# Attention with 32 memory slots and capacity routing on one Trainium2 core: scores and gate products by 64x32 tiles, softmax by groups of up to two units, a written-out order of the front part, and the routing's branch turned round

## The chip, the cores and the metric

The kernel runs on one core of one Trainium2 chip. Its time is the device time of one execution in microseconds. Before the change the median of three runs is 603.41 us (602.47 to 606.62).

## The reference

Eight batches, eight heads, 576 positions, 64 channels, 32 memory slots. First the attention with memory slots, then a mixture of eight experts on its result (4608 rows of 512):

```python
a = exp(phi - max(phi, axis=2)); a = a / sum(a, axis=2)     # over the 576 positions
k_m = einsum('bhsm,bhsd->bhmd', a, k)                       # 32 slots per head
v_m = einsum('bhsm,bhsd->bhmd', a, v)
attn = softmax(q @ k_m.T / 8)                               # over the 32 slots
x = (attn @ v_m) -> rows (b, s) of 8*64 channels
logits = x @ w_gate                                         # 4608 x 8
for (row, expert) in descending order of logit:             # greedy, 576 rows per expert
    if the row is free and the expert has room: assign
out[rows of e] = relu(x[rows of e] @ w1[e]) @ w2[e]
```

## The kernel before

The program has a **front** (attention and routing) and an **expert part**. The front works in eight batches and 18 units. A batch loads phi and the keys and values, takes the exponentials of phi (`ex`), multiplies them with keys and values into 32 slots per head (`kv_`), normalises (`zn`, `zs`), transposes the slots (`kt`), copies them to SBUF (`kb`, `vd`) and multiplies the value slots with the gate weights (`vg`, `vl`), so that logits come with the attention's product. A unit is 256 positions of one batch, or (units 8 and 17) the last 64 positions of four batches. Its steps are: load of the queries (`load_q`), scores on TensorE (`SC`, PE L982), transpose (`T1`, DVE L987), maximum (`MX`, L990), subtraction (`SB`, POOL L993), exponential (`SE`, ACT L996), sums and reciprocal (`SU`, L1000 and L1001), multiplication (`NM`, POOL L1004), transpose (`T2`, DVE L1009), product with the value slots (`AV`, PE L1017), a separate product for the logits of units 13 to 17 (`LG`, `LC`), copies from PSUM (`XC`, ACT L1035), and the write of x to DRAM (`ST`, SP L1044 and L1048).

The scores contract 64 channels. Before, the slots lie in zero-padded tiles of 128 rows (`kbd`), so that both halves of the positions use all 128 rows of the array in 128x32 tiles.

The routing finds thresholds from the logits (L107 to L157), a mask and an assignment (L171 to L178, one-hot `oh`), positions by a scan (L187), and 36 blocks of comparisons `L` (LP on POOL L210, LV on DVE L212, LS on ACT L214), whose product (`ll`, L228) gives row numbers; `ix` (L231, L232) writes them to `idx`. A flag tells whether a slower routing (`rest`) is needed; all engines read it and branch (L292, L293). Then POOL gathers the first expert's 640 rows (L412), five at 128 rows each, and TensorE transposes them (L447) and begins the first expert (L470).

The first expert's weights are loaded in the front as eight tiles of 512 KB: four of w1 (`w1a`, SP L371) and four of w2 (`w2a`, L404). Each is split into two fp32r parts: the high one by a cast on ACT (L374, L405), the low one by a subtraction on POOL (L377, L406). The tiles have four buffers (`st`), and the gathered rows use these too.

What order each engine runs the front in is set by a planner (`build` and `Sched.order`): each step has an engine, a duration, a key and the steps that it needs; a simulated run picks steps by key, and the kernel issues them in the order of the simulated starts. Every engine runs its own queue strictly in order. The expert part has a planner of its own, which the change leaves alone.

Of the kernel before, what the change touches and what calls it, by code (L numbers as in the profile page):

```python
# [66 lines left out]
class Router:  # L67
# [106 lines left out]
    def assign(s):  # L174
# [3 lines left out]
        nc.vector.tensor_tensor(s.oh.rearrange("p e t -> p t e"),m,v[:,:,None].to_broadcast([128,NT,E]),op=ALU.is_ge)  # L178
# [111 lines left out]
    def finish(s):  # L290
        nc=s.nc; tc=s.tc
        rv=nc.values_load(s.flag[0:1,0:1],min_val=0,max_val=E)  # L292
        with tc.If(rv>0):  # L293
# [42 lines left out]
class FFN:  # L336
# [70 lines left out]

    def gather(s,xd,idx,i):
        c=s.cols(0)[i]
        if i%2==0: s.g0=s.sp.tile([128,1024],F32,name="st")  # L410
# [1 line left out]
        s.nc.gpsimd.indirect_dma_start(out=g,out_offset=None,in_=xd,in_offset=bass.IndirectOffsetOnAxis(ap=idx[:,c:c+1],axis=0))  # L412
# [310 lines left out]
def build(X,f,B=8):  # L723
# [9 lines left out]
    for n in range(N):
        T=anch[n]+X['UB'][n]; b,bb,_=units[n]; rem=len(bb)>1
        op('SP',(1.32,3.4),T+X['SC']+X['lq'],lambda n=n:f.load_q(n),[],[('lq',n)],[('Q',X['NQ'],('Q',n))])
        for h in range(2):
# [4 lines left out]
        op('ACT',.68,T+X['SE'],lambda n=n:f.SE(n),[('sb',n)],[('se',n)],[],[('p',n)])
        op('DVE',1.05,T+X['SU'],lambda n=n:f.SU(n),[('se',n)],[('su',n)],[],[('p',n)])
        pool=X['NP']>>(n%2)&1
        op('Pool' if pool else 'DVE',1.13 if pool else .97,T+X['NM'],lambda n=n,e=pool:f.NM(n,e),[('su',n)],[('nm',n)],[],[('p',n)])
        op('DVE',.74,T+X['T2'],lambda n=n:f.T2(n),[('nm',n)],[('t2',n)],[('pTd',len(X['DF']),('pT',n)) if n in X['DF'] else ('pT',2,('pT',n))],[('p',n)])
# [403 lines left out]
```

## Time and profile before

| what | value |
|---|---|
| profiled execution, whole | 603.53 us |
| its span, first to last instruction | 601.8 us |
| mean granted TensorE clock | 0.971 |
| TensorE busy | 546.1 us (91%) |
| VectorE, ScalarE, GpSimd busy | 394.5, 286.9, 257.9 us |
| bytes moved by DMA | 116.58 MB |
| first gather for the first expert | at 172.13 us |
| first product of the first expert | at 181.25 us |

The 1.7 us between span and whole execution lie around the program. Times in the views are microseconds from the first instruction. In a timeline row come the start, the length, the engine, the line, the operation, output and inputs, and in brackets the idle time before it with what ended it. PE is TensorE, DVE VectorE, ACT ScalarE, POOL GpSimd, SP the queue that issues DMAs.

### The profile page before, as it was taken

To read this page: it belongs to the slowest core of one execution; us is meant where nothing else is said; L and a number is where in the kernel's file an instruction comes from. 1 tells how busy PE (TensorE), PEld (TensorE's weight loads), DVE (VectorE), ACT (ScalarE), POOL (GpSimd) and SP (SyncE) were. 2 spreads that over 40 slices of the span, in tenths; PEclk is the share of its full clock that TensorE was granted. 3 is DMA by queue.
4 is the path that set the end of the run, shared out by engine and by line. 5 is a ranking of instruction groups with operands and counts; after the bars stand their busy time and mean duration, and the time that the engine had idled before them with its cause. 6 is when DMAs were issued, how large, how long until landed. Compare 5 with 4: busy or idle time off the path is not lost.

```text
span 601.8 us, 11305 instructions
## 1 busy us (share of the span) xinstructions
PE 546.1 (91%) x4344; PEld 453.7 (75%) x4344; DVE 394.5 (66%) x738; ACT 286.9 (48%) x577; POOL 257.9 (43%) x244
## 2 busy tenths in 40 slices
PE   8988889665867999999899989999999999999996
PEld 3666666463236988998688879889889889989984
DVE  3486866561722251536888958988897898898800
ACT  2375654614302342443557445646646656754511
POOL 6164544863347325559233431542362182282003
PEclk9999999957989799999999989999999999999999
DMA  8999999842129967895861264152346327315002
GB/s 315 421 414 359 409 355 382 301 139 106 36 81 325 316 218 251 295 287 209 245 188 38 69 210 142 53 204 86 114 129 212 97 70 254 96 35 203 1 0 80
DMA packets 48269, 116.58 MB, mean 194 GB/s; under 512 B 6352, under 2 KB 20304, under 8 KB 46160
## 3 DMA queue, kind: packets, MB, share of 16 engines
q1 hardware_dynamic: 41584, 94.29, 45.5%
q0 software_dynamic: 6624, 21.50, 9.8%
q8 instruction: 36, 0.59, 0.4%
q14 instruction: 25, 0.20, 0.1%
HBM read 87.45 MB, written 28.31 MB: 192 GB/s over the span
## 4 chain that ended last, share of the span: by engine, by line
PE 42%; issue 13%; DMA 8%; POOL 4%; ACT 2%; DVE 2%; SPq 1%; POOLq 0%; DVEq 0%; ACTq 0%
PE ph L482 18%; PE ph L501 16%; PE ph L470 5%; DMA xsort<-xu,pi 3%; POOL out L506 2%; PE ph L490 2%; DMA xu<-xd 2%; DMA out<-y,idx 1%; DMA st<-in_moe_w 1%; POOL xsort L431 1%; PE ph L447 1%; SPq L439 1%; DVE w1l L391 1%; DMA g<-xsort 1%; DMA st<-xd,idx 1%
## 5 line engine op out<-in xcount | busy, mean ns | idle before, releaser
L501 PE MATMUL ph<-w2h,hh 128*128 128x512 f32 x256 | 101.5, 397 | 0.0
L501 PE MATMUL ph<-w2h,hl 128*128 128x512 f32 x256 | 101.4, 396 | 0.0
L501 PE MATMUL ph<-w2l,hh 128*128 128x512 f32 x256 | 101.1, 395 | 0.0
L506 POOL DMA_INDIRECT out<-y,idx x32 | 41.0, 1280 | 92.4 <-ACT y L503 86.4
L501 PEld LDWEIGHTS ph<-w2l,hh 128*128 128x128 f32 x256 | 48.1, 188 | 11.7
L501 PEld LDWEIGHTS ph<-w2h,hh 128*128 128x128 f32 x256 | 48.1, 188 | 11.3
L501 PEld LDWEIGHTS ph<-w2h,hl 128*128 128x128 f32 x256 | 48.1, 188 | 11.1
L503 ACT COPY y<-ph 128x512 f32<-128x512 f32 x32 | 18.8, 587 | 64.6 <-PE ph L501 48.4
L431 POOL DMA_INDIRECT xsort<-xu,pi x36 | 35.7, 992 | 27.3 <-DMA xu<-xd 16.8
L482 PE MATMUL ph<-xh,w1h 128*128 128x288 f32 x192 | 41.9, 299 | 3.2 <-ACT p L562 3.1
L383 POOL TENSOR_TENSOR st<-st 128x512 f32<-128x512 f32 x24 | 41.5, 1735 | 7.2 <-ACT s1h L390 2.5
L473 DVE SCALAR_TENSOR_TENSOR hl<-ph,hh 128x288 fp32r<-128x288 f32 x56 | 24.1, 450 | 30.9 <-ACT hh L472 17.2
L383 POOL TENSOR_TENSOR st<-s,st 128x512 f32<-128x512 f32 x12 | 18.7, 1562 | 58.7 <-DVE w1l L391 32.8
L473 DVE SCALAR_TENSOR_TENSOR hl<-cc,hh 128x288 fp32r<-128x288 f32 x72 | 39.8, 573 | 6.1 <-ACT hh L472 5.7
L482 PE MATMUL ph<-xh,w1l 128*128 128x288 f32 x192 | 41.6, 298 | 0.0
L482 PE MATMUL ph<-xl,w1h 128*128 128x288 f32 x192 | 41.2, 296 | 0.0
L472 ACT ACTIVATE hh<-ph 128x288 fp32r<-128x288 f32 x56 | 21.6, 410 | 38.4 <-PE ph L470 15.4
L391 DVE TENSOR_TENSOR w1l<-st,w1h 128x512 fp32r<-128x512 f32 (+1 forms) x24 | 34.5, 1444 | 4.8 <-issue 4.8
L405 ACT CAST w2h<-st 128x1024 fp32r<-128x1024 f32 x32 | 33.4, 1046 | 7.4 <-DMA st<-in_moe_w 6.2
L406 DVE TENSOR_TENSOR w2l<-st,w2h 128x1024 fp32r<-128x1024 f32 x28 | 34.0, 1217 | 4.2 <-ACT w2h L405 3.3
L383 POOL TENSOR_TENSOR s<-st 128x512 f32<-128x512 f32 x12 | 17.2, 1438 | 43.7 <-DMA st<-in_moe_w 39.6
L472 ACT ACTIVATE hh<-cc 128x288 fp32r<-128x288 f32 x72 | 30.3, 443 | 10.1 <-DVE cc L484 10.1
(194 smaller groups left out, 1326.5 us busy)
## 6 DMA issues: line engine op xcount, KB each, us to landing
st<-in_moe_w SPq DMA_DIRECT2D x64, 512.0 KB
kv<-in_kv SPq DMA_DIRECT2D x16, 1161.0 KB
qm<-in_q SPq DMA_DIRECT2D x18, 512.0 KB
xd<-xs SPq DMA_DIRECT2D x16, 512.0 KB
xu<-xd SPq DMA_DIRECT2D x16, 512.0 KB
g<-xsort SPq DMA_DIRECT2D x96, 64.0 KB
pt<-in_phi SPq DMA_DIRECT2D x8, 576.0 KB
xd<-xs SPq DMA_DIRECT2D x8, 128.0 KB
```

The lines of the kernel that those rows point to most:

```text
L383: s.nc.gpsimd.tensor_tensor(o,x,y,op=ALU.subtract if i else ALU.add)
L391: def wlo(s,e,c,i): h,l,x=s.wop(e,c,i); s.nc.vector.tensor_tensor(l,x,h,op=ALU.subtract)
L405: def l2b(s,j): s.nc.scalar.copy(s.w2h[j],s.R2[j])
L406: def l2c(s,j,pool=False): (s.nc.gpsimd if pool or j in WP else s.nc.vector).tensor_tensor(s.w2l[j],s.R2[j],s.w2h[j],op=ALU.subtract)
L431: i=s.nc.gpsimd.indirect_dma_start(out=xs,out_offset=bass.IndirectOffsetOnAxis(ap=pi[:,t:t+1],axis=0),in_=s.X[n][:,a],in_offset=None)
L470: for j in js: nc.tensor.matmul(ph[j][:,:288],w,x[:,2*j+k//2,k%2],start=(i==0),stop=(i==11))
L472: def rh(s,f,j,c): s.nc.scalar.activation(s.hh[:,f,j],c[:,:288],AF.Relu)
L473: def rl(s,f,j,c): s.nc.vector.scalar_tensor_tensor(s.hl[:,f,j],c[:,:288],0.0,s.hh[:,f,j],op0=ALU.max,op1=ALU.subtract)
L482: s.nc.tensor.matmul(c[:,:288],s.W(w,a)[:,k,m],x[:,b,k],start=start and n==0,stop=n==5,skip_group_check=not start); n+=1
L501: nc.tensor.matmul(py,a[:,f,j,o],b,start=(f==0 and q==0),stop=(f==7 and q==2))
L503: def full_y(s,c,py): s.Y[c]=y=s.yp.tile([128,D],F32,name="y"); s.nc.scalar.copy(y,py)
L506: i=s.nc.gpsimd.indirect_dma_start(out=out,out_offset=bass.IndirectOffsetOnAxis(ap=ix,axis=0),in_=s.Y.pop(c)[:n],in_offset=None)
```

## The change

The slots are copied once, unpadded (`kvt`), and scores, gate products and the last 64 rows of phi's product use tiles of 64 rows and 32 columns. `vd` and the padded buffers go. The softmax steps MX, SB, SE, SU, NM and T2 work on groups of one or two units (`GRP`). Some copies and splits move to DVE (`ALT`), the POOL blocks of `L` go (`RV=[27,0,9]`: DVE, POOL, ACT). The loads of w2 now need the last group's NM, and their casts the last group's SE. The planner's order is replaced by a table of 514 numbers. The gathers move into the branch that is taken when the flag is zero, ahead of the large `RV`; twelve warm-up products before the gathered rows go. The core of the diff:

```diff
 class Sched:
+ORDER=(285,286,288,264,289,290,306,291,292,287,293,294,309,73,310,267,
...
+504,510,)
-    AVS=194.9, SU=21.38, NM=60.47, XC=86.9, LO=-19.41, ST=-61.43, EV=11, NP=3, NB=7, NQ=9, NK=2,
+    AVS=194.9, SU=21.38, NM=60.47, XC=86.9, LO=-19.41, ST=-61.43, EV=11, NP=3, NB=6, NQ=8, NK=2,
-    CF=323.04, CB=630.67, NA=2, BD=[1, 2, 3, 5, 7], DF=[13, 14, 15, 16, 17], LG=272.42, LC=-601.61, DA=519.47,
-    DX=160.21, DS=404.52, R0=251.98, RK=-1728.94, W1=-59.3, WH=341.28, WS=227.46, WE=0, W2=-50, WB=100, RV=[22, 6, 8], la=-57.61,
+    CF=323.04, CB=630.67, NA=2, BD=[0, 1], DF=[13, 14, 15, 16, 17], LG=272.42, LC=-601.61, DA=519.47,
+    DX=160.21, DS=404.52, R0=251.98, RK=-1728.94, W1=-59.3, WH=341.28, WS=227.46, NX=3, NU=3, GRP=[[2],[3],[1,0],[5,10],[8,6],[4,12],[11,7],[9],[14,16],[13,15],[17]], ALT=(('xc',2,0),('xc',2,1),('nm',1),('xc',15,1),('xc',17,1),('w1c',1),), W2=-50, WB=100, RV=[27, 0, 9], la=-57.61,
-        op('SP',(1.32,3.4),X['W2']+i,lambda j=j:f.w2a(j),[('w1a',3)],[('w2a',j)],[('st',4,('s2',j))])
-        op('ACT',1.1,X['W2']+X['WB']+i,lambda j=j:f.w2b(j),[('w2a',j)],[('w2b',j)],[],[('s2',j)])
+        op('SP',(1.32,3.4),X['W2']+i,lambda j=j:f.w2a(j),[('w1a',3),('nm',len(X['GRP'])-1)],[('w2a',j)],[('st',4,('s2',j))])
+        op('ACT',1.1,X['W2']+X['WB']+i,lambda j=j:f.w2b(j),[('w2a',j),('se',len(X['GRP'])-1)],[('w2b',j)],[],[('s2',j)])
-        seq=S_.order(X['slack'])
+        seq=S_.fixed(ORDER) if ORDER else S_.order(X['slack'])
...
         def SC(n,hh):
-            for u in range(2):
-                for m,bb in enumerate(bs):
-                    for i in range(4):
-                        nc.tensor.matmul(sc[32*i:32*i+32,u,hh,w*m:w*m+w],KBD[ks[bb]][:,4*hh+i,u,:],qT[:,4*hh+i,w*m:w*m+w],start=True,stop=True)
+            for m,bb in enumerate(bs):
+                for i in range(4):
+                    for u in range(2):
+                        r=slice(64*u,64*u+64); o=128*hh+w*m
+                        nc.tensor.matmul(sc[32*i:32*i+32,u,o:o+w],KVT[ks[bb]][r,0,hh,32*i:32*i+32],qT[r,4*hh+i,w*m:w*m+w],start=True,stop=True)
...
-    def finish(s):
-        nc=s.nc; tc=s.tc
+    def finish(s,rows):
+        nc=s.nc; tc=s.tc; a=s.FIRST; t=s.rt(a,NT)
         rv=nc.values_load(s.flag[0:1,0:1],min_val=0,max_val=E)
-        with tc.If(rv>0):
-            s.rest(4)
-            s.slots()
+        with tc.If(rv<1) as c:
+            s.ix(0,a); rows(); s.RV(a,NT,t)
+        with c.Else():
+            s.rest(4); s.slots(); s.ix(0,a); rows(); s.RV(a,NT,t)
+        s.il=s.ps.tile([128,2,NT-a],F32,name=s.tg[1][0],bufs=s.tg[1][1]); s.nl=0
+        s.ll(range(NT)); s.ix(a,NT)
...
-            r.finish()
-            for c in range(r.FIRST):
-                f.gather(xd, r.idx, c)
-            f.warm(r, 12)
-            r.later()
+            f.rows0()
+            r.finish(lambda: [f.gather(xd, r.idx, c) for c in range(r.FIRST)])
```

The table moves three queues at the end of the front. On POOL, before the change, the last steps ahead of the gathers are these (L406 and L377 are splits of w2 and w1, L993 SB, L1004 NM, L210 the blocks of `L`, L292 and L293 the flag and the branch):

```order
L377 TENSOR_TENSOR w1l_1499<-st_1601,w1h_1498 128x2x512
L993 TENSOR_TENSOR pu2_97<-pu2_97,mx_1869 128x16x32
L406 TENSOR_TENSOR w2l1_1505<-st_1878,w2h1_1501 128x1024
L406 TENSOR_TENSOR w2l3_1507<-st_1901,w2h3_1503 128x1024
L1004 TENSOR_TENSOR pu2_97<-pu2_97,z_1919 128x16x32
L210 TENSOR_SCALAR L_1967<-cb_68,lf_1963 128x128 x6
L292 TENSOR_LOAD flag_77
L293 COMPARE_AND_BRANCH
```

After the change POOL has there (L1019 is NM, L403 and L374 the splits, L411 the gathers):

```order
L1019 TENSOR_TENSOR pu0_90<-pu0_90,z_1645 128x32x32
L1019 TENSOR_TENSOR pu1_91<-pu1_91,z_1665 128x16x32
L403 TENSOR_TENSOR w2l3_1285<-st_1694,w2h3_1281 128x1024
L374 TENSOR_TENSOR w1l_1277<-st_1419,w1h_1276 128x2x512
L374 TENSOR_TENSOR w1l_1277<-st_1638,w1h_1276 128x2x512
L403 TENSOR_TENSOR w2l2_1284<-st_1965,w2h2_1280 128x1024
L374 TENSOR_TENSOR w1l_1277<-st_1959,w1h_1276 128x2x512
L403 TENSOR_TENSOR w2l0_1282<-st_1963,w2h0_1278 128x1024
L403 TENSOR_TENSOR w2l1_1283<-st_1824,w2h1_1279 128x1024
L290 TENSOR_LOAD flag_77
L291 COMPARE_AND_BRANCH
L411 DMA st_1975<-xd_62,idx_75 128x512 x2
```

Seven splits now stand behind the last NM and ahead of the first gather; before, two stood ahead of the last NM and none behind it.

On SP the last rows before the flag were these (L404 loads w2, L1044 and L1048 write x):

```order
L1044 DMA xd_62<-xs_1770 128x1024
L1044 DMA xd_62<-xs_1723 128x1024
L404 DMA st_1878<-in_moe_w2 128x2x512
L404 DMA st_1901<-in_moe_w2 128x2x512
L1044 DMA xd_62<-xs_1894 128x1024
L1044 DMA xd_62<-xs_1903 128x1024
L1044 DMA xd_62<-xs_1867 128x1024
L1048 DMA xd_62<-xs_1982 32x1024 x4
L292 TENSOR_LOAD flag_77
```

and are now (L368 loads w1, L401 w2, L1062 and L1066 write x):

```order
L401 DMA st_1824<-in_moe_w2 128x2x512
L1066 DMA xd_62<-xs_1867 32x1024 x4
L368 DMA st_1959<-in_moe_w1 128x1024
L1062 DMA xd_62<-xs_1814 128x1024
L1062 DMA xd_62<-xs_1837 128x1024
L401 DMA st_1963<-in_moe_w2 128x2x512
L401 DMA st_1965<-in_moe_w2 128x2x512
L290 TENSOR_LOAD flag_77
```

Three loads of weights have moved behind the write of unit 17 (`xs_1867`).

On ACT the end of the front was (L1035 XC, L405 casts of w2, L996 SE, L109 copies for the thresholds, L214 and L215 the blocks of `L`):

```order
L405 CAST w2h1_1501<-st_1878 128x1024
L1035 COPY xs_1903<-av_1905 128x512
L996 ACTIVATE pu2_97<-pu2_97 128x16x32
L405 CAST w2h3_1503<-st_1901 128x1024
L1035 COPY xs_1867<-av_1911 128x512
L1035 COPY xs_1982<-av_1945 128x512
L109 COPY pe_78<-tp_1971 96x128
```

and is now, from the casts on (L402 casts of w2, L371 of w1, L1051 XC), first the piece around the threshold copies and right behind the blocks of `L` the last five casts:

```order
L402 CAST w2h3_1281<-st_1694 128x1024
L371 CAST w1h_1276<-st_1638 128x2x512
L109 COPY pe_78<-tp_1729 96x128
L109 COPY pe_78<-tp_1773 96x128
L114 ACTIVATE j2_1787,nv_1788<-pe_78,cf_67 96x384
```

```order
L215 ACTIVATE L_1780<-LA_1781 128x512
L371 CAST w1h_1276<-st_1755 128x2x512
L402 CAST w2h0_1278<-st_1963 128x1024
L402 CAST w2h2_1280<-st_1965 128x1024
L402 CAST w2h1_1279<-st_1824 128x1024
L371 CAST w1h_1276<-st_1959 128x2x512
```

The last group's SE no longer stands behind a cast of w2; two casts now stand ahead of the second threshold copy, and five behind the blocks of `L`. On DVE the steps behind the last block of `L` are now the copies `XC` of units 15 and 17, one split of w1, the flag, the branch, `ix` and the large `RV`. In the expert part the rows of all engines are the same as before.

More of the change, by code (lines that the diff above doesn't have):

```diff
@@ L88, in begin @@
         s.tg=(pos,il)
-        s.T=ps.tile([128,E],F32,name=T[0],bufs=T[1])
+        s.T=T
         t=lambda sh,n,dt=F32: wk.tile(sh,dt,name=n)
@@ L741, in build @@
[L741 to L745, printed above, removed]
+            op('PE',.9 if rem else .45,T+X['SC']+.5*h,lambda n=n,h=h:f.SC(n,h),[('lq',n)]+[('kb',x) for x in bb]+([('sc',n,0)] if h else []),[('sc',n,h)],[] if h else [('sc',1,('sc',n))],[('Q',n),('sc',n)]+[('KB',x) for x in bb])
@@ new lines, in build @@
+        g,k=grp[n]; w=len(X['GRP'][g])-1; last=k==w
+        op('DVE',.75,T+X['T1'],lambda n=n:f.T1(n),[('sc',n,1)]+([('t1',X['GRP'][g][0])] if k else []),[('t1',n)],[] if k else [('p',X['NU'],('p',g))],[('sc',n),('p',g)])
+        if last:
+            op('DVE',(.73,1.27)[w],T+X['MX'],lambda g=g:f.MX(g),[('t1',x) for x in X['GRP'][g]],[('mx',g)],[],[('p',g)])
+            op('Pool',(1.12,2.2)[w],T+X['SB'],lambda g=g:f.SB(g),[('mx',g)],[('sb',g)],[],[('p',g)])
+            op('ACT',(.68,1.2)[w],T+X['SE'],lambda g=g:f.SE(g),[('sb',g)],[('se',g)],[],[('p',g)])
+            op('DVE',(1.08,1.64)[w],T+X['SU'],lambda g=g:f.SU(g),[('se',g)],[('su',g)],[],[('p',g)])
+            q,d=alt(('nm',g),('Pool',(1.12,2.2)[w]),('DVE',(.97,1.87)[w]))
+            op(q,d,T+X['NM'],lambda g=g,e=q=='Pool':f.NM(g,e),[('su',g)],[('nm',g)],[],[('p',g)])
+            df=X['GRP'][g][0] in X['DF']
+            op('DVE',(.75,1.3)[w],T+X['T2'],lambda g=g:f.T2(g),[('nm',g)],[('t2',g)],[(f'pTd{w}',sum(len(l)==w+1 and l[0] in X['DF'] for l in X['GRP']),('pT',g)) if df else ('pT',2,('pT',g))],[('p',g)])
@@ L850, in front @@
         NB=PRMS['NB']; vs={}; ks={}
-        KBD=[cp.tile([128,8,2,M],F32,name=f"kbd{i}") for i in range(NB)]
-        VBD=[cp.tile([128,2,4,M],F32,name=f"vbd{i}") for i in range(2)]
-        AL=[cp.tile([128,2,4,M],F32,name=f"al{i}") for i in range(2)]
-        PU=[cp.tile([128,16,M+1],F32,name=f"pu{i}") for i in range(3)]
+        KVT=[cp.tile([128,2,2,128],F32,name=f"kvt{i}") for i in range(NB)]
+        PU=[cp.tile([128,2,16,M+1],F32,name=f"pu{i}") for i in range(PRMS['NU'])]
         VB=[cp.tile([128,2,264],F32,name=f"vb{i}") for i in range(NB)]
@@ new lines, in pz, with wide, MX, SB @@
+        def pz(g): return U[g,'z'][:,:len(GRP[g])].rearrange("p w a m -> p (w a) m")
+        def wide(t,g): return t[:,:16*len(GRP[g])]
+        def MX(g):
+            assert all((n,'t1') in OK for n in GRP[g])
+            U[g,'mx']=mx=w3.tile([128,32],F32,name="mx")
+            nc.vector.reduce_max(wide(mx,g),pz(g)[:,:,:M],axis=AX.X)
+        def SB(g):
+            p=pz(g)[:,:,:M]; OK[g,'sb']=1
+            nc.gpsimd.tensor_tensor(p,p,wide(U.pop((g,'mx')),g)[:,:,None].to_broadcast([128,16*len(GRP[g]),M]),op=ALU.subtract)
@@ L1010, in AV, with T2 @@
+        def T2(g):
+            p=pz(g)[:,:,:M]; assert OK[g,'n']; U.pop((g,'z')); w=len(GRP[g])
+            df=GRP[g][0] in PRMS['DF']
+            pT=w3.tile([128,w,2,2,128],F32,name=f"pTd{w}",bufs=NDF[w]) if df else w3.tile([128,2,2,2,128],F32,name="pT",bufs=2)[:,:w]
+            nc.vector.transpose(pT.rearrange("p w u a (b t) -> p (w u a b) t",t=M),p)
+            for k,n in enumerate(GRP[g]): U[n,'pT']=pT[:,k]
         def AV(n,u):
@@ L1038, in ST @@
             units[n][3](U[n,'x'])
+        GRP=PRMS['GRP']; grp={n:(g,k) for g,l in enumerate(GRP) for k,n in enumerate(l)}
+        NDF={w:sum(len(l)==w and l[0] in PRMS['DF'] for l in GRP) for w in (1,2)}
         units=[]; first={}
```

170 lines of the change are left out of this document (82 added, 88 removed).

## Prediction, made before the changed kernel was run

> **What bounds the kernel now.** I read the busy times first, then stretches of the span, then the rows where nothing is full.
>
> ```profile
> PE 546.1 (91%) x4344; PEld 453.7 (75%) x4344; DVE 394.5 (66%) x738; ACT 286.9 (48%) x577; POOL 257.9 (43%) x244
> 20.00:100.00 80.00, 67.93 (x1292) 49.62 (x1284) 59.34 (x146) 44.37 (x82) 37.53 (x59) 1.00 0.99 387
> 100.00:172.00 72.00, 48.90 (x498) 30.10 (x497) 37.43 (x97) 26.14 (x49) 37.99 (x28) 0.85 0.43 153
> 202.00:602.00 400.00, 387.40 (x2215) 344.10 (x2213) 283.19 (x462) 203.71 (x424) 155.18 (x118) 0.99 0.46 150
> ```
>
> The columns of a stretch are its length, the busy time of PE, PEld, DVE, ACT and POOL, the granted clock, the DMA share and GB/s. The 91% of PE is an average over three stages. From 20 to 100 us the DMA engines are full (share 0.99, 387 GB/s), and PE has 12 us to spare. From 202 us to the end PE is full (387.40 of 400), and there the change moves no row. From 100 to 172 nothing is full (PE 48.90 of 72, DMA 0.43): a chain of waits. What this chain gets shorter, the kernel gains. So I ask when the first gather starts, and let the expert part follow it as a block.
>
> The chain before, in order of time:
>
> ```profile
> 101.91 0.38 SPq L883 DMA_DIRECT2D qm<-in_q  x1
> 112.14 0.38 SPq L404 DMA_DIRECT2D st<-in_moe_w  x1
> 118.18 1.04 ACT L405 CAST w2h<-st 128x1024 fp32r<-128x1024 f32 x1 [2.22 <-DMA st<-in_moe_w]
> 119.31 2.35 POOL L406 TENSOR_TENSOR w2l<-st,w2h 128x1024 fp32r<-128x1024 f32 x1 [1.36 <-ACT w2h L405]
> 121.61 3.08 POOL L1004 TENSOR_TENSOR pu<-pu,z 128x512 f32<-128x512 f32 x3
> 125.74 0.70 DVE L987 STREAM_TRANSPOSE pu<-sc 128x512 f32<-128x512 f32 x1
> 139.03 4.65 POOL L406 TENSOR_TENSOR w2l<-st,w2h 128x1024 fp32r<-128x1024 f32 x2 [8.69 <-ACT w2h L405]
> 144.72 0.71 DVE L1009 STREAM_TRANSPOSE pTd<-pu 128x512 f32<-128x512 f32 x1 [3.73 <-POOL pu L1004]
> 155.96 1.38 DVE L178 TENSOR_TENSOR oh<-msk,vmax 128x288 f16<-128x288 f32 x1
> 161.62 3.54 DVE L212 TENSOR_TENSOR L<-cb,lh 128x512 f16<-128x512 f16 x5
> 171.56 1.32 DVE L222 TENSOR_TENSOR R<-cb,h 128x1116 f16<-128x1116 f16 x1 [3.81 <-DVEq L293]
> 172.13 1.80 POOL L412 DMA_INDIRECT st<-xd,idx  x1 [5.35 <-issue]
> 181.25 1.86 PE ph L470 x12
> ```
>
> The last queries are issued at 101.91, but their transpose T1 runs only at 125.74, because a cast of w2 waits for its load (118.18) and its split stands on POOL ahead of three NM. The last T2 ends at 145.43 (144.72 + 0.71), behind two more splits. The blocks of `L` end at 165.16 (161.62 + 3.54), 19.7 us later. DVE then spends 3.81 us in the branch, POOL's first gather starts at 172.13, and the first expert product at 181.25, 9.12 us behind it.
>
> **The change part by part.**
>
> *Bytes ahead of the last queries.* Both rows name 512 KB a transfer:
>
> ```profile
> st<-in_moe_w SPq DMA_DIRECT2D x64, 512.0 KB
> xd<-xs SPq DMA_DIRECT2D x16, 512.0 KB
> ```
>
> SP had 10 writes of x and 4 loads of w1 ahead of the last query load, and has now 8 and 1, but also `cf` (0.27 MB). That is 5 x 0.524 - 0.27 = 2.35 MB less, at 387 GB/s 6.1 us: the issue moves from 101.91 to about 95.8. From issue to use a load took 6.0 us (112.14 to the cast at 118.18) or 10.3:
>
> ```profile
> 92.93 4.79 SPq L371 DMA_DIRECT2D st<-in_moe_w  x4
> 103.27 1.04 ACT L374 CAST w1h<-st 128x1024 fp32r<-128x1024 f32 x1 [1.82 <-DMA st<-in_moe_w]
> ```
>
> So the queries land between 102 and 106; I take 104, and with 1.1 us for their scores (1.08 in the row under rival A) and a hop, T1 runs from 105.5.
>
> *The last group's softmax* (group of one unit) no longer has a w2 step ahead of it. DVE runs behind T1, with the last wide group between:
>
> ```profile
> 128.12 0.64 DVE L990 TENSOR_REDUCE mx<-pu 128x16 f32<-128x512 f32 x1
> 140.00 0.70 DVE L1000 TENSOR_REDUCE z<-pu 128x16 f32<-128x528 f32 x1 [5.85 <-ACT pu L996]
> 140.74 0.25 DVE L1001 RECIPROCAL z<-z 128x16 f32<-128x16 f32 x1
> 143.63 1.06 POOL L1004 TENSOR_TENSOR pu<-pu,z 128x512 f32<-128x512 f32 x1
> 123.71 1.10 DVE L102 SCALAR_TENSOR_TENSOR pq<-no,lg 128x96 f32<-128x96 f32 x1
> 133.28 0.24 DVE L101 SCALAR_TENSOR_TENSOR pq<-no,lg 128x80 f32<-128x80 f32 x1
> 155.47 0.45 DVE L177 TENSOR_REDUCE vmax<-msk 128x36 f32<-128x288 f32 x1
> ```
>
> T1 0.70, MX 0.64, a wide SU (twice 0.70, and 0.25), its own SU 0.95, a wide T2 (1.40), T2 0.71, two logit steps of about 0.4 and four first threshold steps (0.24 each in the quiet of 133 us, 1.10 for one of them while POOL ran NM; 1.0 to 3.1 for the four): 8.6 to 10.7. I take 10, hence T2 ends near 116 (112 to 118) in place of 145.43: **-29.4**. A group of two saves only the gap between two instructions; I price it at nothing, since most of it lies where DMA is full. So do the scores by 64x32 tiles, the dropped `vd` and zero fills, and the moved copies. Without that cover they can't cost more than PE's 12 us of idle from 20 to 100.
>
> *Routing* took 19.7 us. Five more blocks of `L` on DVE at 3.54/22 each: +0.8. The one-hot step ran 1.38 with its output written across experts, and is written in order now; it may keep its 1.38 or come down to the 0.45 of the step ahead of it, which reads as many elements: 0 to -0.9, I take -0.5. On ACT two casts now stand ahead of the second threshold copy, and their loads are issued behind the last NM: 0 to +5, I take +2.5, the middle. So 22.5, and the blocks of `L` end near 138.5 (-26.6).
>
> *What stands between that and the gather now.* Three loads (w1, w2, w2) stand on SP behind the write of unit 17. That write waits for the copy `XC` of unit 17 on DVE, behind the last block of `L`, and for its product on PE:
>
> ```profile
> 117.29 1.03 PE L1017 MATMUL av<-vb,pTd 128*128 128x256 f32 x4
> 148.19 1.94 PE L1017 MATMUL av<-vb,pTd 128*32 128x256 f32 x16
> 140.79 0.60 ACT L1035 COPY xs<-av 128x512 f32<-128x512 f32 x1
> 137.90 1.05 ACT L405 CAST w2h<-st 128x1024 fp32r<-128x1024 f32 x1
> 150.84 1.72 SPq L1048 DMA_DIRECT2D xd<-xs  x4
> 174.24 3.66 DMA st<-xd,idx
> ```
>
> Product of unit 15 1.03, of unit 17 1.94, copy 0.60 and 0.8 for the hops: 4.4, to 142.9. SP issues nine DMAs, the write's four (1.72) and five at 0.43: to 146.8. The last load lands 6.0 later (between the 3.66 of a gather's transfer and 10.3): 152.8. Its cast, 1.05: 153.9. POOL has four splits from there (w2l2, w1l, w2l0, w2l1) at 4.65/2 = 2.33: 163.2. Then the flag and the branch. POOL stands in order, so all this is **ahead of the first gather**, whose rows have long been known. Behind POOL, the expert's transposes, and all PE work, wait.
>
> *The branch.* Before, the gather followed DVE's 3.81 us. Now the gathers' side is the one that the code runs into; flag and compare may cost nothing like that, but also up to 3.81 on POOL itself. I take 0.6, a loaded flag without a jump, nearer to zero since the way to the gathers was the jump before and isn't now. Gather at **163.8** against 172.13: **-8.3**. DVE's own saving is worth nothing while POOL is last. The jump over the other side comes behind the gathers now; at 3.81 or less it is hidden by the 9.12 that the first rows take.
>
> *The clock.* The twelve warm products go, and PE then waits about 25 us for the rows:
>
> ```profile
> 123.00:137.00 14.00, 11.96 (x40) 10.39 (x41) 7.06 (x16) 2.02 (x4) 7.34 (x5) 0.51 0.35 108
> 171.00:174.00 3.00, 2.69 (x7) 1.04 (x8) 2.41 (x3) 0.00 (x0) 1.80 (x1) 0.50 0.03 8
> 174.00:195.00 21.00, 16.25 (x138) 13.74 (x137) 5.31 (x14) 3.61 (x9) 14.40 (x15) 0.99 0.82 276
> ```
>
> After a wait the clock was 0.51 and 0.50; the warm products took it back to 0.99 before the expert's first. Without them the expert begins at half: the 1.86 us of its first twelve products would double, and perhaps the 1.6 behind them; 0 to +3.4, I take +1.3, since PE also waits in these first microseconds. The Trainium skill, "TensorE: Matmul & The Clock Gate", Part 1 (The HAM clock gate), has it that the array starts at half clock after an idle window of about 3.4 us and rises after about as much busy time; by it the loss is at most 1.7 us, an estimate. The rows 0.50 and 0.99 agree with it.
>
> Sum: -8.3 + 1.3 = **-7.0**. The profiled execution took 603.53 (span 601.8), the median 603.41, so I need no correction: **596.5**.
>
> **The rivals.**
>
> *A. Tile modes drain PE in the front.* Scores change tile shape against their neighbours more often, some 70 switches more. If each holds PE for one product's time, 0.27 (the median of the first row below, 272 ns), PE gets 19 us more and has 12 of slack; T1 of the last unit slips by up to 7, and the chain behind passes it on: 598 to 604. Against it:
>
> ```profile
> L982 PE MATMUL sc<-qm,kbd x768: 196/272/298, 26.4 to 116.2; 128*32 128x128 f32 x128, 128*32 128x32 f32 x64
> 110.57 1.08 PE L982 MATMUL sc<-qm,kbd 128*32 128x128 f32 x32
> 111.58 1.13 PE L1017 MATMUL av<-vb,pTd 128*128 128x256 f32 x4
> ```
>
> The scores end at 111.65, after the next product, in another tile shape, has started (111.58): no gap at this switch. The Trainium skill, "TensorEngine Tiling (Array Packing)", Key Properties, says that changing the tile mode drains the array; this row shows no such drain. With other slips of the front by 2 to 7 us counted here: 0.22.
>
> *B. Slower: the loads land in a backlog.* Place: the last queries, and the three loads behind the write of unit 17. Price: if both take 10.3 in place of 6.0, as the row at 92.93 did, the gather comes 8.6 later than forecast, at 172.4: 605.1. It turns to a loss once the two slips sum to 7.0, and is over 1% slower (609.5) from 13.0 on, when either lands after 12.5 us. For it: the DMA share was 0.99 until 100 us, where the last queries are loaded. Against it: it is 0.43 in the stage of the late loads. Chance 0.12. The other open ends (the branch at 3.81, casts ahead of the thresholds at 5, the clock at 3.4: +3.2, +2.5, +2.1) go the same way and widen the range.
>
> *C. POOL doesn't hold the gather, or for less.* If the loads come out early enough that the splits are done by the time the row numbers are, the gather follows 6 us behind 138.5: -27 + 1.3, some 578. With half of the splits early, 582 to 592. For it: five of the seven splits' weights could be loaded by 130. Against it: the write of unit 17 stands ahead of three loads in SP's order. Chances 0.04 and 0.12.
>
> **How the numbers follow.** Forecast 0.50 (592.5 to 598.5), A 0.22 (598 to 604), B 0.12 (603.4 to 610), C 0.16. The range leaves out 578, the lower half of 582 to 592 and most of B: 588.5 to 604. A measurement of this kernel can tell about 1% (6.0 us) from no change. Faster by more, under 597.4: C, and some 0.40 of the forecast's 0.50: 0.56. Slower by more, over 609.4: the end of B with 0.07. Within: 0.37.
>
> **What would show it.** Right: the last T2 near 116, the last blocks of `L` near 138, the first gather in one row behind a run of four splits on POOL from 154 to 163, idx written 15 us before it; a granted clock near 0.5 at the first expert product. A: a fuller PE than 68 of 80 in 20 to 100, and the last T1 after 110. B: casts of w2 waiting for DMA past 158. C: a gather that waits for idx on DVE. The prediction is wrong at its root if rows behind the first expert product move, for I take 420 us there as a block.

## The result, and the profile after: 1.4% slower

The changed kernel takes 613.83 us (median of 14 runs) against 604.84 for the kernel before in the same runs. Some executions of after, the one profiled first among them, ran longer at a lower granted clock, so the ratio of 1.0136 [1.0109, 1.0162] leaves them out, and the rows of after shown here are those of its execution in the experiments (610.07 us, span 608.3; ratio there 1.0103 [1.0024, 1.0183]). The forecast was 596.5 us with a range of 588.5 to 604.

First the busy times of the page and the stretches of the span of the kernel after (length, busy PE, PEld, DVE, ACT, POOL, clock, DMA share, GB/s):

```profile
PE 527.3 (87%) x4368; PEld 440.7 (72%) x4368; DVE 397.6 (65%) x694; ACT 274.4 (45%) x546; POOL 247.1 (41%) x216
20.00:100.00 80.00, 71.32 (x1522) 47.14 (x1520) 53.87 (x108) 38.39 (x62) 48.42 (x59) 0.96 0.99 385
117.00:128.00 11.00, 3.37 (x49) 2.37 (x48) 10.22 (x21) 2.44 (x5) 6.95 (x3) 0.65 0.48 186
144.00:174.00 30.00, 6.10 (x64) 3.65 (x61) 9.47 (x12) 4.53 (x5) 9.63 (x5) 0.50 0.49 161
```

PE has 18.8 us less to do in all (546.1 to 527.3), and the span is longer. From 20 to 100 DMA is still what is full. From 144 to 174 no engine is busy for a third of the time: the chain of waits is still there, in another place.

The chain of the kernel after, in order of time:

```profile
107.45 0.70 DVE L999 STREAM_TRANSPOSE pu<-sc 128x512 f32<-128x512 f32 x1
115.90 0.69 DVE L1024 STREAM_TRANSPOSE pTd<-pu 128x512 f32<-128x512 f32 x1
118.86 2.35 POOL L403 TENSOR_TENSOR w2l<-st,w2h 128x1024 fp32r<-128x1024 f32 x1 [4.67 <-ACT w2h L402]
118.94 2.37 DVE L100 TENSOR_TENSOR no<-lg,rv 128x80 f32<-128x80 f32 x1
121.16 4.64 POOL L374 TENSOR_TENSOR w1l<-st,w1h 128x1024 fp32r<-128x1024 f32 x2
121.41 2.19 DVE L101 SCALAR_TENSOR_TENSOR pq<-no,lg 128x80 f32<-128x80 f32 x1
123.52 2.38 DVE L102 SCALAR_TENSOR_TENSOR pq<-no,lg 128x80 f32<-128x80 f32 x1
127.22 0.42 PE L107 MATMUL tp<-id,pq 128*96 128x128 f32 x1 [7.28 <-DVE pq L102]
127.42 0.22 DVE L124 TENSOR_REDUCE mm<-mg 128x16 f32<-128x64 f32 x1
141.09 2.55 DVE L212 TENSOR_TENSOR L<-cb,lh 128x768 f16<-128x768 f16 x3
144.06 1.92 PE L1033 MATMUL av<-vb,pTd 128*128 128x256 f32 x4
148.81 0.69 DVE L1051 COPY xs<-av 128x512 f32<-128x512 f32 x1 [2.11 <-PEq L291]
149.57 2.93 SPq L1066 DMA_DIRECT2D xd<-xs  x4
150.75 0.16 DVE L232 SCALAR_TENSOR_TENSOR idx<-i,av 128x5 int32<-128x5 f32 x1
155.44 1.49 SPq L401 DMA_DIRECT2D st<-in_moe_w  x2
163.08 1.99 ACT L402 CAST w2h<-st 128x1024 fp32r<-128x1024 f32 x2 [0.41 <-DMA st<-in_moe_w]
164.20 2.34 POOL L403 TENSOR_TENSOR w2l<-st,w2h 128x1024 fp32r<-128x1024 f32 x1 [38.40 <-ACT w2h L402]
168.80 4.63 POOL L403 TENSOR_TENSOR w2l<-st,w2h 128x1024 fp32r<-128x1024 f32 x2
173.60 1.17 POOL L411 DMA_INDIRECT st<-xd,idx  x1 [0.17 <-POOL w2l L403]
```

The last T2 ends at 116.59, 28.8 us earlier than before. DVE's blocks of `L` end at 143.64, 21.5 earlier (before, the last block was one of POOL's and ended at 166.79, 1.6 us behind DVE's). The row numbers are written at 150.91, and the gather that needs them starts 22.7 us later, behind four splits that had waited 38.40 us for the last loads: 173.60, 1.5 us **later** than before. All of the front's gain is lost between 116 and 174. From the end of the last T2 to the step `mm` it is 10.8 us. Before it was 1.9:

```profile
147.36 0.22 DVE L124 TENSOR_REDUCE mm<-mg 128x16 f32<-128x64 f32 x1
```

The other loss is behind the first product. PE's and ACT's rows of the kernel after:

```profile
182.54 0.80 PE L469 MATMUL ph<-xh,w1h 128*128 128x288 f32 x4
184.24 0.60 PE L446 MATMUL ph<-id,st 128*128 128x128 f32 x4
186.28 0.60 PE L446 MATMUL ph<-id,st 128*128 128x128 f32 x4
194.01 0.58 ACT L453 CAST xh<-ph 128x512 fp32r<-128x512 f32 x1 [11.36 <-remote]
198.37 0.58 ACT L453 CAST xh<-ph 128x512 fp32r<-128x512 f32 x1 [3.77 <-remote]
199.01 1.33 PE L469 MATMUL ph<-xh,w1h 128*128 128x288 f32 x4 [12.13 <-ACT xh L453]
```

PE stands still for 12.13 us, from 186.88, until ACT has cast the fourth and the fifth row tile (`xh`). ACT waited 11.36 us for the fourth, whose transpose is the PE row at 184.24: its products behind it run on without a gap, and yet ACT starts 9.2 us after its end. The name "remote" says only that no local row explains the release. In the trace's events the semaphore that ACT waits for here, one that PE raises with the last of these products, goes up at 193.99 and 198.34. For the tiles without such a wait it goes up 0.01 to 0.02 us behind PE's row (p_a0: row end 182.50, semaphore 182.51). So the delay lies on PE's side, in the product itself (the ends of PE's rows are modelled) or in its signal, and not in ACT. Nor does a load of code explain it: from 174 to 206 no packet runs on the DMA queues for instructions. Before, these casts ran at 183.58 and 186.20 without such a wait:

```profile
183.58 0.59 ACT L454 CAST xh<-ph 128x512 fp32r<-128x512 f32 x1 [2.22 <-PE ph L447]
186.20 0.59 ACT L454 CAST xh<-ph 128x512 fp32r<-128x512 f32 x1 [2.03 <-PE ph L447]
```

The kernel before has late signals too, but shorter ones: the semaphore goes up 4.6 and 5.9 us behind the PE rows that end at 188.70 and 190.30, and ACT waits 6.20 and 2.19 us for "remote". In the first 26 us behind the first product PE is busy 13.87 us in the kernel after and 22.58 in the kernel before.

From the first product to the end of the span it is 425.8 us, and was 420.6. So of the 8.7 us of PE work that are missing in those 26 us, 3.5 are made up later. The spans differ by 6.5: +1.5 to the gather, -0.2 from there to the first product (8.94 against 9.12), +5.2 behind it.

### The profile page after: what moved, and what is told of

Read it like the earlier page. It is cut to its first block, busy times and chain, and to the rows that moved or that the text cites. A ratio compares the mean times of both kernels' runs of the same rounds, so it can differ in the third digit from the quotient of the medians.

```text
span 619.6 us, 11230 instructions
## 1 busy us (share of the span) xinstructions
PE 541.0 (87%) x4368; PEld 450.9 (73%) x4368; DVE 398.2 (64%) x694; ACT 274.4 (44%) x546; POOL 247.1 (40%) x216
## 4 chain that ended last, share of the span: by engine, by line
PE 37%; issue 14%; DMA 8%; POOL 6%; DVE 3%; another core or an unknown queue 2%; ACT 2%; SPq 1%; POOLq 0%; ACTq 0%; DVEq 0%
PE ph L481 17%; PE ph L500 14%; PE ph L469 4%; DMA out<-y,idx 3%; POOL out L505 2%; DMA xsort<-xu,pi 2%; DMA st<-in_moe_w 2%; PE ph L489 2%; POOL st L380 2%; DVE w1l L388 1%; POOL w2l L403 1%; DMA xu<-xd 1%; POOL xsort L430 1%; DMA st<-xd,idx 1%
## 5 line engine op out<-in xcount | busy, mean ns | idle before, releaser
L505 POOL DMA_INDIRECT out<-y,idx x32 | 39.2, 1225 | 106.0 <-ACT y L502 100.1
L502 ACT COPY y<-ph 128x512 f32<-128x512 f32 x32 | 18.8, 586 | 67.8 <-PE ph L500 51.2
L430 POOL DMA_INDIRECT xsort<-xu,pi x36 | 36.6, 1016 | 23.8 <-DMA xu<-xd 13.8
L380 POOL TENSOR_TENSOR st<-s,st 128x512 f32<-128x512 f32 x12 | 18.8, 1563 | 61.4 <-DVE w1l L388 36.1
L402 ACT CAST w2h<-st 128x1024 fp32r<-128x1024 f32 x32 | 33.3, 1046 | 20.3 <-DMA st<-in_moe_w 19.3
L388 DVE TENSOR_TENSOR w1l<-st,w1h 128x512 fp32r<-128x512 f32 (+1 forms) x24 | 36.5, 1529 | 4.9 <-DMA st<-in_moe_w 4.9
L403 DVE TENSOR_TENSOR w2l<-st,w2h 128x1024 fp32r<-128x1024 f32 x28 | 34.0, 1218 | 3.4 <-ACT w2h L402 3.0
L481 PEld LDWEIGHTS ph<-xh,w1h 128*128 128x128 f32 x192 | 32.2, 195 | 4.4 <-ACT p L561 3.7
L481 PE MATMUL ph<-xh,s1h 128*128 128x288 f32 x144 | 31.8, 302 | 4.2 <-ACT xh L397 3.4
## 6 DMA issues: line engine op xcount, KB each, us to landing
xd<-xs SPq DMA_DIRECT2D x8, 128.0 KB
```

Of the source, the lines that this page charges most:

```text
L380: s.nc.gpsimd.tensor_tensor(o,x,y,op=ALU.subtract if i else ALU.add)
L388: def wlo(s,e,c,i): h,l,x=s.wop(e,c,i); s.nc.vector.tensor_tensor(l,x,h,op=ALU.subtract)
L402: def l2b(s,j): s.nc.scalar.copy(s.w2h[j],s.R2[j])
L403: def l2c(s,j,pool=False): (s.nc.gpsimd if pool or j in WP else s.nc.vector).tensor_tensor(s.w2l[j],s.R2[j],s.w2h[j],op=ALU.subtract)
L430: i=s.nc.gpsimd.indirect_dma_start(out=xs,out_offset=bass.IndirectOffsetOnAxis(ap=pi[:,t:t+1],axis=0),in_=s.X[n][:,a],in_offset=None)
L481: s.nc.tensor.matmul(c[:,:288],s.W(w,a)[:,k,m],x[:,b,k],start=start and n==0,stop=n==5,skip_group_check=not start); n+=1
```

## The experiments

Each experiment has one profile and a ratio to the kernel before in the same runs. Times in the profile, in us: end of the last T2, of DVE's blocks of `L`, of the splits ahead of the gather; first gather; first product; from there to the end; span. (Before and in x3 POOL has blocks of `L` too, which end at 166.79 and 152.61.) The runs lie on several chips, on which the kernel before took 599.9 to 602.7 us, so ratios are compared and not times.

| kernel | T2 | `L` | splits | gather | product | to the end | span | ratio to before |
|---|---|---|---|---|---|---|---|---|
| before | 145.4 | 165.2 | 143.7 | 172.1 | 181.3 | 420.6 | 601.8 | 1 |
| after (a0) | 116.6 | 143.6 | 173.4 | 173.6 | 182.5 | 425.8 | 608.3 | 1.0103 [1.0024, 1.0183] |
| x1, loads first | 117.3 | 151.0 | 145.7 | 167.3 | 177.5 | 434.1 | 611.6 | 1.0103 [1.0028, 1.0178] |
| x1b, loads and writes first | 118.4 | 152.0 | 146.7 | 161.1 | 172.8 | 421.1 | 593.9 | 0.9899 [0.9805, 0.9993] |
| x2, no table | 127.7 | 154.0 | 140.8 | 155.7 | 166.3 | 428.9 | 595.2 | 0.9870 [0.9798, 0.9942] |
| x2_old, no table, old branch | 128.0 | 153.5 | 142.3 | 158.7 | 169.5 | 421.3 | 590.8 | 0.9871 [0.9796, 0.9945] |
| x3, before with w2's waits | 126.3 | 151.0 | 140.1 | 162.3 | 170.2 | 417.1 | 587.3 | 0.9849 [0.9799, 0.9898] |
| p_a0, three splits on DVE | 116.3 | 140.6 | 170.5 | 170.6 | 179.6 | 418.0 | 597.6 | 1.0030 [0.9988, 1.0072] |
| h2, hold of sorted rows | 118.2 | 145.2 | 175.5 | 175.7 | 184.9 | 416.3 | 601.2 | 1.0008 [0.9969, 1.0047] |
| x6, splits on DVE | 118.9 | 140.5 | 152.5 | 153.1 | 163.7 | 414.9 | 578.6 | 0.9680 [0.9619, 0.9740] |

**Do the late loads hold the gather?** The kernel after as it is:

> The changed kernel again, on the chip of the runs beside it. Theory Q (the queue): the gather follows POOL's four late splits, some 20 us behind the row numbers. It expects here first gather near 175 to 181 us with idx written by 160, and 609 to 615 us. Theory C (the clock): what is lost is lost ahead of that, where PE runs at half clock behind the last T2; it expects the same time, and a half clock from about 103 to 145 us in an undisturbed profile too. Theory E (the expert's start): 10 us are lost behind the first expert product, where PE stood still from 193.5 to 205.5 us; it expects this gap here again.

The gather starts at 173.60, 22.7 us behind `idx`, as theory Q says. Theory C's half clock right behind 103 isn't there: the clock is 1.00 from 103 to 117. The gap of theory E is there again, 12.13 us.

Then the three loads ahead of the last writes on SP, their casts between the copies on ACT, and all splits on POOL. SP's rows:

```diff
+L1062 DMA xd<-xs 128x1024
+L401 DMA st<-in_moe_w 128x2x512
+L368 DMA st<-in_moe_w 128x1024
+L401 DMA st<-in_moe_w 128x2x512 x2
+L1062 DMA xd<-xs 128x1024
+L1066 DMA xd<-xs 32x1024 x4
 L1062 DMA xd<-xs 128x1024 x2
-L401 DMA st<-in_moe_w 128x2x512
-L1066 DMA xd<-xs 32x1024 x4
-L368 DMA st<-in_moe_w 128x1024
-L1062 DMA xd<-xs 128x1024 x2
-L401 DMA st<-in_moe_w 128x2x512 x2
```

> Of the order table only the places of first-expert weight steps move: three late loads (w1, w2, w2) and one more w2 load go ahead of the last four writes of x on SP, their casts between the copies ahead of the blocks of L on ACT, all splits on POOL (one comes over from DVE). Theory Q: POOL is free when the row numbers come; the gather then waits for the writes of unit 17 to land, near 165 in place of 180.8: 16 us less than the changed kernel, 594 to 600. Theory C: the splits only stood in a shadow, under 4 us less. Theory E: the gap behind the first product stays and the time falls by what the gather moves.

And the same with the products of units 15 and 17 ahead of `ll` on PE, and their copies on ACT, so that the writes come early too:

```diff
-... ALT=(('xc',2,0),('xc',2,1),('nm',1),('xc',15,1),('xc',17,1),),
+... ALT=(('xc',2,0),('xc',2,1),('nm',1),),
```

> As the run with the loads first, and the products of the second halves of units 15 and 17 go ahead of the products of L on PE, their copies to ACT between and behind its blocks of L, so that the last writes of x don't wait for the routing. Theory Q: the gather follows the row numbers by some 3 us or the last write's landing, near 158 to 160: 20 us less than the changed kernel, 589 to 596. Theory C: no more than 4 us less. Theory E: the gap behind the first product stays.

In x1 the splits are done at 145.7, 28 us earlier, and the gather gains 6.3 of them. The time gains nothing: the ratio is 1.0103 again, where 594 to 600 us had been expected, and 610.78 were measured. What the gather gained, x1 lost behind its first product (434.1 us against 425.8), where ACT waits 13.11 us for the fourth tile. The gather's row in x1:

```profile
167.32 1.17 POOL L411 DMA_INDIRECT st<-xd,idx  x1 [21.62 <-DMA xd<-xs]
```

POOL has been free for 21.62 us, and the gather waits for the last write of x to land. So loads and writes are two gates in one queue: SP. With both early (x1b) the gather comes at 161.1, and the kernel is 1% faster than before, with an interval that ends just under 1. But part of that is lost on DVE. Rows of x1b:

```profile
136.64 2.57 POOL L403 TENSOR_TENSOR w2l<-st,w2h 128x1024 fp32r<-128x1024 f32 x1 [6.91 <-ACT w2h L402]
137.52 2.15 DVE L178 TENSOR_TENSOR oh<-msk,vmax 128x288 f16<-128x288 f32 x1
141.78 4.88 POOL L403 TENSOR_TENSOR w2l<-st,w2h 128x1024 fp32r<-128x1024 f32 x2
142.06 2.31 DVE L191 SCALAR_TENSOR_TENSOR cs<-sc,cf 1x8 f32<-1x8 f32 x1
144.98 1.72 DVE L202 TENSOR_SCALAR h<-pi 128x36 int32<-128x36 int32 x1
161.09 1.17 POOL L411 DMA_INDIRECT st<-xd,idx  x1 [14.43 <-DMA xd<-xs]
```

The same three steps take 0.67, 0.15 and 0.18 in the kernel after, where POOL is idle beside them. A step that reads eight numbers (L191) takes 2.31 us beside a split. Not every step suffers: a reduction (L105) that starts at 127.57, beside another split of x1b, takes its usual 0.45.

**What do the steps beside the splits cost?** The kernel after with three of its seven POOL splits on DVE, ahead of the threshold steps:

```diff
-... ('w1c',1),),
+... ('w1c',1),('w1c',3),('w1c',2),('w2c',3)),
-        op('Pool',2.45,X['W2']+X['WB']+i,lambda j=j:f.w2c(j),[('w2b',j)],[('w2c',j)],[],[('s2',j)])
+        q,w=alt(('w2c',j),('Pool',2.45),('DVE',1.25))
+        op(q,w,X['W2']+X['WB']+i,lambda j=j,d=q=='DVE':f.w2c(j,d),[('w2b',j)],[('w2c',j)],[],[('s2',j)])
```

> The changed kernel with three of its seven late splits, those that run on POOL beside the threshold steps, on DVE itself ahead of these steps. Theory P: three DVE steps that take 2.2 to 2.4 us beside POOL go back to 0.25, 6.5 us less, and the splits add 3 x 1.22 = 3.7: from the last T2 to the step mm 8 us in place of 10.8, gather 3 us earlier, 604 to 608. If the steps are slow for another reason, 14 us from T2 to mm and 611 to 615.

DVE's rows there:

```profile
119.56 1.22 DVE L403 TENSOR_TENSOR w2l<-st,w2h 128x1024 fp32r<-128x1024 f32 x1
122.09 0.24 DVE L100 TENSOR_TENSOR no<-lg,rv 128x80 f32<-128x80 f32 x1
122.44 0.24 DVE L101 SCALAR_TENSOR_TENSOR pq<-no,lg 128x80 f32<-128x80 f32 x1
122.59 0.23 DVE L102 SCALAR_TENSOR_TENSOR pq<-no,lg 128x80 f32<-128x80 f32 x1
124.35 0.22 DVE L124 TENSOR_REDUCE mm<-mg 128x16 f32<-128x64 f32 x1
```

The three steps fall from 6.94 us together to 0.71. Three splits of about 1.22 come to DVE, net -2.6; `mm` comes 3.07 earlier and the gather 3.0. That part of the cause is shown. The 12 us gap behind the first product is gone too (more on that below), so the kernel gains more than the gather's 3.0 us.

**Table or the rest?** Everything but the table, the same with the branch as before, and the kernel before with nothing but w2's two waits:

```diff
-ORDER=(285,286,288,264,...
+ORDER=()
```

> The change with everything but its table: the planner's own order in its place (tiles, groups, copies, needs of w2, turned branch as in the change). It puts all w2 loads ahead of the last writes and all splits of POOL ahead of the row numbers. Theory Q: the loss was in the table; first gather some 5 us behind the blocks of L, 585 to 598. Theory C: if 64x32 tiles and groups starve or slow PE, the half clock from 103 us on stays and the time stays above 603. Theory E: the gap behind the first product stays whatever the order.

```diff
+        s.ix(0,a)
-        with tc.If(rv<1) as c:
-            s.ix(0,a); rows(); s.RV(a,NT,t)
-        with c.Else():
-            s.rest(4); s.slots(); s.ix(0,a); rows(); s.RV(a,NT,t)
+        with tc.If(rv>0):
+            s.rest(4); s.slots(); s.ix(0,a)
+        rows(); s.RV(a,NT,t)
```

> The change with the planner's order and with the branch as it was before: row numbers ahead of the flag, the gathers behind the jump. With the turned branch the gather started 1.7 us behind the last block of L. Theory Q (the branch counts only where POOL isn't last): here the jump stands in the way, gather some 5 to 7 us behind the blocks of L, 3 to 5 us more than with the turned branch: 598 to 602. If the turned branch saves nothing, 595 to 597.

```diff
-...lambda j=j:f.w2a(j),[('w1a',3)],[('w2a',j)],[('st',4,('s2',j))])
+...lambda j=j:f.w2a(j),[('w1a',3),('nm',17)],[('w2a',j)],[('st',4,('s2',j))])
-...lambda j=j:f.w2b(j),[('w2a',j)],[('w2b',j)],[],[('s2',j)])
+...lambda j=j:f.w2b(j),[('w2a',j),('se',17)],[('w2b',j)],[],[('s2',j)])
```

> The kernel before with one part of the change: w2's loads wait for the last NM, its casts for the last SE, and the planner orders anew. Theory Q (the stretch from the last queries to the first gather is a chain of queues): the last T2 comes 20 us earlier or more, POOL's splits end before the row numbers are known, the first gather near 155 to 160 in place of 172: 588 to 598 us. If the tiles, groups and the table were the source of the gain of 29 us at T2, this run stays within 3 us of 603.

Without the table the change is 1.3% faster; the table costs 1.0103/0.9870, 2.4%. The two waits alone bring as much as the whole change without its table, waits included (0.9849 against 0.9870, with overlapping intervals). So tiles, groups, copies and the branch together add nothing that these runs can tell; what each does by itself wasn't tested. Rows of x3:

```profile
125.03 2.24 SPq L404 DMA_DIRECT2D st<-in_moe_w  x3
130.86 9.26 POOL L406 TENSOR_TENSOR w2l<-st,w2h 128x1024 fp32r<-128x1024 f32 x4 [5.31 <-ACT w2h L405]
162.25 1.87 POOL L412 DMA_INDIRECT st<-xd,idx  x1 [9.63 <-issue]
```

The planner puts the loads of w2 ahead of the last writes, and the four splits end at 140.1, 22 us ahead of the gather. The table had moved loads behind writes.

The branch: in x2 the gather comes 1.7 us behind the blocks of `L`, in x2_old 5.2. The gather's row in x2, then a row of DVE and the gather's in x2_old:

```profile
155.74 1.39 POOL L411 DMA_INDIRECT st<-xd,idx  x1 [14.95 <-DVE idx L232]
158.05 1.32 DVE L222 TENSOR_TENSOR R<-cb,h 128x1116 f16<-128x1116 f16 x1 [3.79 <-DVEq L292]
158.72 1.68 POOL L411 DMA_INDIRECT st<-xd,idx  x1 [16.42 <-DVEq L292]
```

So the turned branch is worth some 3.5 us at the gather where POOL is free. The time shows none of it (0.9870 and 0.9871; x2_old had been expected 3 to 5 us longer): x2 loses 7.6 us more behind its first product. In the kernel after, POOL itself is last, so the branch has nothing to gain there.

**The gap behind the first product.** POOL issues the five gathers, five more for the second expert (L419) and, right behind them, the indirect transfers of the sorted rows (`xsort`, L430). One small POOL instruction that reads the fifth row tile's `xh` and `xl` holds all later indirect transfers (h, where it stands in `run` behind that tile), or only those of the sorted rows (h2, whose edit is shown):

```diff
         ... sort, first tile
+        if t==0: s.nc.gpsimd.tensor_tensor(s.hp[:,7,1,1,:],s.xl[:,3,1,224:256],s.xh[:,3,1,224:256],op=ALU.subtract)
```

> The changed kernel with one small operation on POOL ahead of its indirect transfers for the second expert and for the sorted rows: it reads the low part of the first expert's last row tile, so that these transfers start behind it. Theory E (the first expert waits 12 us because of the transfers that POOL issues meanwhile): the gap of 12 us behind the first products goes to under 4, and the kernel gains 5 to 8 us: 602 to 606. Theory Q alone: the gap stays, 608 to 611. If the wait comes from something else in the transfers, it stays too.

> The changed kernel with the hold of POOL only ahead of the sorted-row transfers; the second expert's five row gathers go as before. If the sorted-row transfers make the first expert's cast of the fourth row tile wait (20.4 us behind the gather in the changed kernel, 11.4 with everything held), it comes near 12 here, and less is given back at 290 us: 600 to 605. If the second expert's row gathers do, the cast stays near 18 to 20, and 607 to 610.

The first hold (603.71 us, 1.0042 [1.0004, 1.0081]) and the second take the gap away. ACT's row of h2 for the fourth tile, and POOL's first transfer of sorted rows:

```profile
188.12 0.59 ACT L454 CAST xh<-ph 128x512 fp32r<-128x512 f32 x1 [3.13 <-PE ph L447]
191.54 0.25 POOL L430 TENSOR_TENSOR hp<-xl,xh 128x32 fp32r<-128x32 f32 x1 [3.40 <-DVE xl L456]
192.26 1.01 POOL L431 DMA_INDIRECT xsort<-xu,pi  x1 [0.47 <-issue]
```

ACT waits 3.13 us in place of 11.36, and the part behind the first product takes 416.3 in place of 425.8. So in the kernel after, as far as these runs show, the gap needs those transfers at that time. But they are not enough: p_a0 issues them as early, 12.8 us behind its first gather (the kernel after: 12.7), and has no gap. Rows of p_a0:

```profile
182.54 0.59 ACT L453 CAST xh<-ph 128x512 fp32r<-128x512 f32 x1 [2.88 <-PE ph L446]
183.40 1.00 POOL L430 DMA_INDIRECT xsort<-xu,pi  x1 [0.30 <-issue]
```

What else it takes stays open. The wait was seen in x1 (13.11 us) and x2 (7.96) too, not in x2_old or x6. Full DMA engines aren't enough for it either: in x2_old their share is 1.02 from 170 to 180, where the transfers of sorted rows run too (from 171.94), and the two casts wait only 3.60 and 1.63 us.

**A version with both gates earlier.** x1b with seven of the eight splits on DVE and the last one on POOL, and w2's last two loads behind the writes:

```diff
-... ALT=(('xc',2,0),('xc',2,1),('nm',1),),
+... ALT=(('xc',2,0),('xc',2,1),('nm',1),('w1c',3),('w1c',2),('w1c',1),('w1c',0),('w2c',3),('w2c',1),('w2c',2)),
```

> The changed kernel with none of the eight splits but one on POOL: two in gaps of DVE's routing steps, the rest on DVE behind the blocks of L, loads in two pieces around them, the last copies on ACT. DVE steps of 0.25 us ran 2.2 to 2.4 beside POOL's splits. Theory P (POOL's splits slow the routing on DVE, 6.5 us in the changed kernel, more with the loads first): blocks of L end near 138 in place of 143.7 (152 with the loads first), first gather near 150: 583 to 590. Theory Q without P: the routing is as long as before, gather at 156 to 160, 590 to 597.

It takes 581.09 us, 3.2% less than before. Its rows:

```profile
121.21 0.24 DVE L100 TENSOR_TENSOR no<-lg,rv 128x80 f32<-128x80 f32 x1
140.78 2.69 SPq L1067 DMA_DIRECT2D xd<-xs  x4
143.57 0.94 SPq L401 DMA_DIRECT2D st<-in_moe_w  x2
149.10 2.35 POOL L403 TENSOR_TENSOR w2l<-st,w2h 128x1024 fp32r<-128x1024 f32 x1 [32.64 <-ACT w2h L402]
153.09 1.98 POOL L411 DMA_INDIRECT st<-xd,idx  x1 [1.64 <-POOLq L291]
```

The threshold steps are at 0.24, the last writes and loads out by 144.5, and the gather comes 20.5 us earlier than in the kernel after. It still stands behind a split on POOL, the last one, and behind the branch. With the hold of h added it gains nothing (583.62 us, 0.9757 [0.9678, 0.9837]):

> The same with the hold of POOL's later transfers. Theory E: 5 to 8 us less than without the hold; otherwise the same.

## Why the prediction was wrong

**The path to the gather was right; three of its terms were too small, and the part behind it was no block.** Forecast was a gather behind a run of four splits on POOL, with `idx` written some 15 us before. That is what the rows show, but at 173.60 and not at 163.8. The terms:

| step of the prediction | forecast | measured | off by |
|---|---|---|---|
| end of the last T2 | 116 | 116.59 | +0.6 |
| routing, T2 to the end of `L` | 22.5 | 27.1 | +4.6 |
| to the copies of units 15 and 17 | 4.4 | 5.9 | +1.5 |
| SP's nine issues | 3.9 | 7.4 | +3.5 |
| last load and its cast | 7.1 | 7.3 | +0.2 |
| four splits | 9.3 | 9.2 | -0.1 |
| flag and branch | 0.6 | 0.2 | -0.4 |
| gather | 163.8 | 173.6 | +9.8 |

*Routing* is the first step that failed. I had four threshold steps ahead of the last T2, at 0.24 each or 1.10 for one, and looked for the open cost on ACT (+2.5). The casts on ACT cost nothing: the second threshold copy runs at 127.68, right behind its product. In the order on DVE three sets of threshold steps stand **behind** T2 (before, one), and one set runs beside splits: 6.94 us for three steps of 0.24. From T2's end to `mm` it is 10.8 us, against 1.9 before, 8.0 in p_a0 and 4.6 in x6. From `mm` on, routing is 1.6 us shorter than before. The row that told it stood in the prediction: 1.10 for a step beside an NM of 1.05. I read it as a dearer step, when it was a step that ends with POOL's instruction, and a split is 2.35 long. The Trainium skill, "SBUF — State Buffer", Who interferes with whom, has the rule: a DVE instruction with two SBUF inputs contends with a GpSimd instruction that reads SBUF, and the port pair that the two share is an exclusive lock. The rows agree: the three steps end at 121.31, 123.60 and 125.90, the splits at 121.21, about 123.5 and 125.80. *The one-hot step* came down to 0.67 (forecast 0.88).

*The copies of units 15 and 17* took 5.9 in place of 4.4. Unit 15's product was priced at 1.03, from a row at full clock, and took 1.92 at a clock of 0.54 (144 to 147). And the sum had one copy where two follow each other with a product between, at 0.69 each on DVE.

*The nine issues* were priced at 0.43 each behind a write of four. The write of four took 2.93 (before 1.72), and the nine 7.4. I had taken each DMA's price from a quiet row; nothing here tells why these were slower.

*"The expert part as a block"* failed, as the prediction named for its root: +5.2 us, a gap of 12.1 us where the kernel before had shorter ones, less what is made up later. Its cause is shown in part (the sorted rows' transfers, by h2) and open in part (p_a0).

*The clock* cost nothing at the first products: PE's first four take 0.80 as before, and the granted clock is 1.00 from 182.5 to 185, not near 0.5; I had +1.3. In h2 the same four took 1.33, so a loss of this kind can occur, at half a microsecond. But it cost where I hadn't looked: PE idles 7.28 us while DVE stands beside the splits, the clock is 0.65 from 117 to 128 and 0.50 from 144 to 174, and unit 15's product is 0.9 us longer for it. Half clock after an idle stretch agrees with the Trainium skill, "TensorE: Matmul & The Clock Gate", Part 1, which the prediction named.

**The rivals.** A (drains at mode changes) falls: PE is fuller, 71.32 of 80, but the last T1 runs at 107.45, 2 us later than forecast, and T2 on time. B had the direction, and its sign is there (a cast of w2 waits for DMA until 161.62, past 158), but not the reason: its loads took 6 to 7 us from issue to cast, not 10.3; the slip came ahead of them, in DVE, PE and SP. C's mechanism is what x2 shows: splits done at 140.8, and a gather that waits for `idx`. That x6 takes 581.09 us, near C's "some 578", is luck: its gather comes at 153.1 where C had 144.5, and its part behind the first product takes 414.9 where the forecast had 420. x1 shows what C left out: it named only the loads, and the writes of x are a second gate.

**Sum.** Forecast -8.3 + 1.3 = -7.0; measured +1.5 - 0.2 + 5.2 = +6.5. Of the 13.5 us between them 9.8 come from the terms ahead of the gather, 5.2 from behind the first product, and -1.5 from the clock and the first rows. (The 6.5 are from one execution of each kernel; the ratio of 1.0136 makes it 8.2 us of 604.84.) The range held open the bounds of single terms, but not that three of them would slip together, nor anything behind the first product.

## What to carry to other kernels

When work moves from one stage of an engine to a later one, list what runs **beside** it on the other engines: here seven splits left the softmax and met the routing, and DVE steps of 0.24 us became 2.3. A load placed behind a write on one queue inherits every wait of that write, so put a weight's load ahead of writes that end late, and the writes that the next stage reads ahead of the loads that it doesn't. And test a large rewrite part by part: two added needs were worth as much as the whole of it without its table.
